# Whole float32 scores in twelve heads instead of eight, V's high parts on ACT, and the keys' low parts on GpSimd in an attention and mixer kernel

## The chip, the cores and the metric

The kernel runs on one core of one Trainium2 chip. Its time is the device time of one execution in microseconds (us); the time before is the median of three runs. One profiled execution was traced, and all spans, busy times and waits are from that execution. In the profile's rows PE is TensorE's matmuls, PEld its weight loads, DVE is VectorE, ACT is ScalarE, POOL is GpSimd, and SP is the engine whose queue issues the DMAs.

## The reference

Eight batches of eight heads go through block-causal attention (576 positions, 64 wide, blocks of 64), and the result x through a token mixer of rank 32 and a two-layer channel mixer:

```
scores = q @ k.T / 8;  masked where block_i < block_j
attn   = softmax(scores);  x = attn @ v          # heads side by side: 576 x 512 per batch
u      = x + (x.T @ U @ V).T
out    = u + relu(u @ w_ch1) @ w_ch2             # w_ch1 512 x 2048, w_ch2 2048 x 512
```

All inputs are float32. U, V, w_ch1 and w_ch2 arrive as 64-bit words and are converted on the chip.

## The kernel before

**Two ways to multiply.** A float32 matmul on PE runs as two passes, and the trace shows two MATMUL records for each. A matmul in the type float32r is one pass with a coarser mantissa. To keep accuracy, an operand is split into a high part (a copy to float32r) and a low part (the operand minus its high part), and several float32r products are summed in PSUM.

**Attention, head by head.** `split_qk` (lines 855 to 892) fetches q and k of one head, transposed, into `raw` (two buffers, so that a buffer serves every second head). Heads below FS = 8 use `raw` as it is: ACT multiplies the keys by 1/8 in place (line 874), and `softmax` makes the scores with whole float32 matmuls (line 931). From head 8 on, q and k are fetched twice, into both halves of the partitions (lines 859 and 861). ACT copies q's high part (line 877) and k's, scaled (line 878). GpSimd subtracts q's high part in the upper half (line 880). DVE multiplies k by 1/8 again and subtracts its high part into `k2` (line 885), and a DMA copies q's high part into `q2` (line 892). The scores are then two float32r matmuls a tile (lines 935 and 936). The mask is in the upper halves of q2 and k2, put there once by line 867 while heads FS-2 and FS-1 are prepared.

The scores of a head fill five tiles of 576, 448, 320, 192 and 64 columns. DVE takes the maxima (line 949), ACT the exponentials with their sums (line 960), and GpSimd scales by the inverse sums (line 986). PE transposes (line 1019). Heads below FP = 10 multiply with V in whole float32 (line 1061). Later heads split the transposed scores (lines 996 and 1038) and use V in parts: `split_v` makes the high part on GpSimd (line 904) and the low part there too (line 907), and line 1077 multiplies. `mix` (from line 1089) adds the token mixer after each second head.

**The weights.** `split64` converts 20 pieces of U, V, w1 and w2 during the first heads: one ACT pass, four DVE passes (lines 331, 332, 337 and 345), then a high part on ACT (line 360) and a low part on GpSimd (line 361).

**The channel mixer.** `ffn_chunk` multiplies chunks of 288 tokens: line 465 for the first product and line 488 for the second, into two PSUM banks (`bf`), with ACT (line 470) and DVE (line 473) between them. Its matmuls have the lowest priority and are placed where attention leaves PE free, from head 10 on. The first two chunks run in two turns, each with half of the weights. After the last head come the rest of the chunks and then the block products (line 659).

**What sets the order.** All work is added to a `Plan` as tasks with an engine, an estimated duration, a priority and buffers. `issue` runs them through a list scheduler and writes each engine's instructions in the order that comes out; each engine then works strictly in that order. Tasks with the mark `port`, and all of GpSimd's, are never planned at the same time as each other. Head h has priorities from 1000 h on, its preparation comes 900 earlier than the head before it, and the last pieces of the weights have 9000 to 16000, so that one comes about with each head from 9 to 16. When durations or engines of tasks change, the whole order behind them changes.

Of the kernel before, what the change touches and what calls it, by code (L numbers as in the profile page):

```python
# [12 lines left out]
AF = mybir.ActivationFunctionType  # L13
ALU = mybir.AluOpType
# [3 lines left out]
S = 576  # L18
# [9 lines left out]
SCALE = 0.125  # L28
# [15 lines left out]

FP = 10

FS = 8

PB = (1, 1, 1, 2, 2)

# [189 lines left out]
def _act(n, sbuf=False):  # L240
    return (93 if sbuf else 52) + 0.833 * n


def _dve(n):
    return 69 + 1.042 * n
# [9 lines left out]
def attention_then_mixer(  # L255
# [10 lines left out]
    nc = tc.nc  # L266
# [8 lines left out]
    add = plan.add  # L275

    def f32(ap):
        return ap.bitcast(F32)
# [525 lines left out]
    for r in raw_r:  # L804
# [3 lines left out]
        for x, fill in ((qi, 1.0), (ki, NEG)):  # L808
            nc.gpsimd.affine_select(
                out=x[:, :, 1, :], in_=x[:, :, 1, :], pattern=[[-1, 4], [0, 64]], compare_op=ALU.not_equal,  # L810
# [44 lines left out]
    def split_qk(h, pr):  # L855
        raw, q1, k1, q2, k2 = (r[h % 2] for r in (raw_r, q1_r, k1_r, q2_r, k2_r))

        def fetch():
            nc.sync.dma_start(out=raw[0:64, :], in_=qk[h])
            if h >= FS:  # L860
                nc.sync.dma_start(out=raw[64:P, :], in_=qk[h])
# [9 lines left out]
        if h < FS:  # L871
# [3 lines left out]
            )  # L875
            return
        add("ACT", _act(S, True), pr, lambda: nc.scalar.copy(q1.ap, raw[:, 0:S]), [raw], [q1])
        add("ACT", _act(S, True), pr, lambda: nc.scalar.activation(k1.ap, raw[:, S : 2 * S], AF.Copy, scale=SCALE), [raw], [k1])
        add(
            "POOL", 1380, pr, lambda: nc.gpsimd.tensor_sub(q1[64:P, :], raw[64:P, 0:S], f32(q1[64:P, :])),  # L880
            [raw, q1], [q1],
        )
        add(
            "DVE", _dve(S), pr,
            lambda: nc.vector.scalar_tensor_tensor(
                out=k2[0:64, :], in0=raw[0:64, S : 2 * S], scalar=SCALE, in1=f32(k1[0:64, :]),
                op0=ALU.mult, op1=ALU.subtract,
            ),
            [raw, k1], [k2], port=True,
        )  # L890

        add("SP", 600, pr, lambda: nc.sync.dma_start(out=f32(q2[0:64, :]), in_=f32(q1[0:64, :])), [q1], [q2], after=DL)
# [1 line left out]
    def split_v(h, pr):  # L894
        s = h % 2
        raw, vs = vr_r[h // 2 % 2], vs_r[s]
        if s == 0:
            add("SP", 910, pr, lambda: nc.sync.dma_start(out=raw.ap, in_=v[h // 2]), writes=[raw], after=DL)
        if h < FP:
            return  # L900
        hi, lo = vs[:, :, 0:64], vs[:, :, 64:P]
        add(
            "POOL", 430, pr,
            lambda: nc.gpsimd.tensor_scalar(out=hi, in0=raw[:, s], scalar1=1.0, scalar2=1.0, op0=ALU.mult, op1=ALU.mult),
            [raw], [vs],
        )
        add("POOL", 820, pr, lambda: nc.gpsimd.tensor_sub(lo, raw[:, s], f32(hi)), [raw, vs], [vs])
# [249 lines left out]
    for h in range(NH):  # L1157
        pr = 1000.0 * h
# [79 lines left out]
```

## Time and profile before

| what | us |
|---|---|
| median of 3 runs | 1201.78 (1198.8 to 1202.18) |
| profiled execution, device time | 1201.04 |
| profiled execution, span from first to last instruction | 1199.2 |

The profile's first two parts, its groups of instructions and its views by stretch are read as follows. Busy time of an engine is the time in which at least one of its instructions ran. A row of a group gives line, engine, operation, tiles (out<-in), shape and count, then busy us and the mean ns of one, then the idle time just before these instructions and what ended it. The view of one line gives the shortest, median and longest duration in ns. In the timeline a row has the start, the duration, the instruction, and in brackets the idle time before it. A row of waits gives the waiting instruction, what it waited for, the total us, how often, and the longest.

### The profile page before, as it was taken

Reading aid. Unit: us, or ns where it says so; the run is one execution under the profiler, and the core shown is the slowest. Engines: PE = TensorE matmul, PEld = TensorE weight load, DVE = VectorE, ACT = ScalarE, POOL = GpSimd, SP = SyncE. Lnnn points to the kernel's source line nnn. Section 1 sums busy time; section 2 is a strip of 40 time slices with the busy share of each in tenths; the row PEclk is TensorE's granted clock in tenths of the full one; section 3 lists DMA queues with packets and bytes.
Section 4 is the critical chain, followed back from the end, with each engine's and each line's share of the span. In section 5 each row is a group of like instructions: output and inputs, shape, how many; then the busy total and the mean of one; then the engine's idle time right before and its main releaser. Section 6 shows DMA issues by size and latency. Waiting matters only on the chain.

```text
span 1199.2 us, 25106 instructions
## 1 busy us (share of the span) xinstructions
PE 1169.1 (97%) x8970; PEld 1123.6 (94%) x8970; DVE 980.7 (82%) x2061; ACT 734.0 (61%) x1822; POOL 426.3 (36%) x588
## 2 busy tenths in 40 slices
PE   7989998999999999999999999999999999999998
PEld 5657888999999999999999999999999999999998
DVE  6879899888988898888887488425989889889887
ACT  6878686777878787878786344213544544544443
POOL 4558766665656566665654112210000000000000
PEclk9999999999999999999999999999999999999999
DMA  4465656535364535354532343211231231231221
GB/s 127 146 172 155 188 166 166 139 97 156 81 171 108 144 104 153 101 158 106 144 98 70 104 147 111 81 54 49 72 119 49 72 119 49 72 119 60 60 80 40
DMA packets 76428, 132.13 MB, mean 110 GB/s; under 512 B 9040, under 2 KB 53072, under 8 KB 76304
## 3 DMA queue, kind: packets, MB, share of 16 engines
q1 hardware_dynamic: 76304, 130.53, 38.8%
q8 instruction: 71, 1.16, 0.4%
q14 instruction: 53, 0.43, 0.1%
HBM read 92.75 MB, written 29.49 MB: 102 GB/s over the span
## 4 chain that ended last, share of the span: by engine, by line
PE 79%; DVE 11%; ACT 4%; issue 2%; DMA 2%; SPq 0%; POOL 0%; ACTq 0%; DVEq 0%; POOLq 0%
PE bb L659 29%; PE bf L465 10%; PE bf L488 10%; PE ba L1019 7%; PE ba L1077 5%; PE bg L465 4%; PE bg L488 4%; DVE mx L949 2%; DVE pl L1038 2%; ACT p L960 2%; PE ba L935 2%; PE ba L936 2%; PE ba L1061 1%; PE ba L1116 1%; PE ba L1102 1%
## 5 line engine op out<-in xcount | busy, mean ns | idle before, releaser
L986 POOL TENSOR_SCALAR p<-p,rv 128x192 f32<-128x192 f32 (+4 forms) x320 | 181.0, 580 | 150.5 <-DVE rv L977 92.7
L659 PE MATMUL bb<-hh,w1l 128*128 128x288 f32 x704 | 170.1, 295 | 0.0
L659 PE MATMUL bb<-hh,w1h 128*128 128x288 f32 x704 | 169.4, 295 | 0.0
L960 ACT ACTIVATE p<-ba,mx 128x448 f32<-128x448 f32 (+3 forms) x248 | 114.3, 466 | 22.2 <-DVE mx L949 18.9
L1019 PE MATMUL ba<-ident,p 128*128 128x128 f32 x768 | 123.5, 275 | 2.2 <-DVE pw L994 0.7
L1038 DVE TENSOR_TENSOR pl<-ba,ph 128x512 fp32r<-128x512 f32 x216 | 114.0, 550 | 11.7 <-ACT ph L996 9.2
L659 PE MATMUL bb<-hl,w1h 128*128 128x288 f32 x576 | 123.0, 295 | 0.1
L659 PEld LDWEIGHTS bb<-hh,w1l 128*128 128x128 f32 x704 | 122.9, 190 | 0.0
L659 PEld LDWEIGHTS bb<-hh,w1h 128*128 128x128 f32 x704 | 121.9, 188 | 0.0
L488 PE MATMUL bf<-hh,w2h 128*128 128x288 f32 x392 | 121.2, 309 | 0.0
L488 PE MATMUL bf<-hl,w2h 128*128 128x288 f32 x392 | 116.4, 297 | 0.0
L488 PE MATMUL bf<-hh,w2l 128*128 128x288 f32 x392 | 115.6, 295 | 0.0
L996 ACT CAST ph<-ba 128x512 fp32r<-128x512 f32 x216 | 100.5, 493 | 23.1 <-PE ba L1019 18.3
L447 POOL TENSOR_TENSOR ul<-ur,uh 128x288 fp32r<-128x288 f32 x72 | 63.3, 907 | 129.7 <-PE bf L465 72.6
L613 ACT CAST hh<-hb 128x576 fp32r<-128x576 f32 x98 | 65.9, 672 | 60.6 <-PE bb L659 58.1
L949 DVE TENSOR_REDUCE mx<-ba 128x1 f32<-128x448 f32 (+3 forms) x248 | 94.1, 407 | 10.0 <-PE ba L936 5.4
L1019 PEld LDWEIGHTS ba<-ident,p 128*128 128x128 f32 x768 | 90.5, 141 | 7.9 <-issue 4.5
L880 POOL TENSOR_TENSOR q<-raw,q 64x576 fp32r<-64x576 f32 x56 | 82.6, 1475 | 29.1 <-issue 9.2
L659 PEld LDWEIGHTS bb<-hl,w1h 128*128 128x128 f32 x576 | 91.9, 188 | 0.4 <-DVE hl L614 0.4
L1077 PE MATMUL ba<-ph,vs 128*128 128x256 f32 (+3 forms) x432 | 90.7, 263 | 0.1
L465 PE MATMUL bf<-uh,w1l 128*128 128x288 f32 x392 | 80.8, 303 | 0.0
L488 PEld LDWEIGHTS bf<-hh,w2l 128*128 128x128 f32 x392 | 74.9, 191 | 0.2
(167 smaller groups left out, 3288.1 us busy)
## 6 DMA issues: line engine op xcount, KB each, us to landing
raw<-in_qk_dram SPq DMA_DIRECT2D x120, 288.0 KB, 4.4
st<-in_w_dram SPq DMA_DIRECT2D x32, 512.0 KB, 3.6
o_d<-ot SPq DMA_DIRECT2D x72, 144.0 KB, 2.1
vr<-in_v_dram SPq DMA_DIRECT2D x32, 320.0 KB, 3.4
ur<-u_d SPq DMA_DIRECT2D x64, 144.0 KB, 3.0
whole<-o_d SPq DMA_DIRECT2D x32, 288.0 KB, 3.2
out_dram<-whole SPq DMA_DIRECT2D x32, 288.0 KB, 2.2
ur<-u_d SPq DMA_DIRECT2D x30, 288.0 KB, 3.2
```

The lines of the kernel that those rows point to most:

```text
L465: nc.tensor.matmul(ps[:, :T], w()[wn][:, k, fs], m[k].ap, start=(i == 0), stop=(i == len(ops) - 1))
L488: nc.tensor.matmul(ps[:, :T], w()[wn][:, f, ms], hs[f][x].ap, start=(i == 0), stop=(i == len(ops) - 1))
L613: add("ACT", _act(2 * T, True), E, lambda: nc.scalar.copy(h.ap, x[0]()), [x[1]], [h])
L659: nc.tensor.matmul(bank[:, i, :T], x()[:, w(k)], p.ap[:, k, :], start=first and n == 0, stop=last and n == len(ops) - 1)
L880: "POOL", 1380, pr, lambda: nc.gpsimd.tensor_sub(q1[64:P, :], raw[64:P, 0:S], f32(q1[64:P, :])),
L949: lambda i=i, at=at: nc.vector.tensor_reduce(out=mx[: P if i else 64, i : i + 1], in_=view(i, at), op=ALU.max, axis=AX.XY if wide else AX. ...
L960: nc.scalar.activation(out.rearrange("p (j k) -> p j k", j=2) if wide else out, view(i, at), AF.Exp, bias=mx[:rows, i : i + 1], accum_out= ...
L986: lambda x=x, rows=rows, i=i: nc.gpsimd.tensor_scalar(out=x, in0=x, scalar1=rv[:rows, i : i + 1], scalar2=1.0, op0=ALU.mult, op1=ALU.mult),
L996: add("ACT", _act(n), pr, lambda: nc.scalar.copy(out(), inp()), reads, writes)
L1019: nc.tensor.transpose(out=bank[:, a : a + P], in_=pt_r[i][h % PB[i]][:, j * P : (j + 1) * P], identity=perm.ap)
L1038: "DVE", _dve(m), pr, lambda: nc.vector.tensor_sub(pl[:, low], bank[:, :m], f32(ph[:, low])), [bank, bh], [bl]
L1077: nc.tensor.matmul(bank[0 : c.stop, a:n], vs[:, j, c], x[:, _at(g, j)], start=(i == 0), stop=(i == len(ops) - 1))
```

## The change

Three things are changed. First, FS goes from 8 to 12: heads 8 to 11 also take whole float32 scores from `raw`, and the mask is copied while heads 10 and 11 are prepared. Second, in the heads from 12 on ACT multiplies the keys by 1/8 in place in `raw`, as it does in the early heads, then copies the high part; the low part is now a plain subtraction, and GpSimd does it instead of DVE. Third, V's high part is an ACT copy and not a GpSimd multiplication by one. Lines behind 903 stand one line higher than before.

```diff
-FS = 8
+FS = 12
...
         add("ACT", _act(S, True), pr, lambda: nc.scalar.copy(q1.ap, raw[:, 0:S]), [raw], [q1])
-        add("ACT", _act(S, True), pr, lambda: nc.scalar.activation(k1.ap, raw[:, S : 2 * S], AF.Copy, scale=SCALE), [raw], [k1])
+        add(
+            "ACT", _act(S, True), pr,
+            lambda: nc.scalar.activation(raw[:, S : 2 * S], raw[:, S : 2 * S], AF.Copy, scale=SCALE), [raw], [raw],
+        )
+        add("ACT", _act(S, True), pr, lambda: nc.scalar.copy(k1.ap, raw[:, S : 2 * S]), [raw], [k1])
         add(
             "POOL", 1380, pr, lambda: nc.gpsimd.tensor_sub(q1[64:P, :], raw[64:P, 0:S], f32(q1[64:P, :])),
             [raw, q1], [q1],
         )
         add(
-            "DVE", _dve(S), pr,
-            lambda: nc.vector.scalar_tensor_tensor(
-                out=k2[0:64, :], in0=raw[0:64, S : 2 * S], scalar=SCALE, in1=f32(k1[0:64, :]),
-                op0=ALU.mult, op1=ALU.subtract,
-            ),
-            [raw, k1], [k2], port=True,
+            "POOL", 1380, pr, lambda: nc.gpsimd.tensor_sub(k2[0:64, :], raw[0:64, S : 2 * S], f32(k1[0:64, :])),
+            [raw, k1], [k2],
         )
...
         add(
-            "POOL", 430, pr,
-            lambda: nc.gpsimd.tensor_scalar(out=hi, in0=raw[:, s], scalar1=1.0, scalar2=1.0, op0=ALU.mult, op1=ALU.mult),
+            "ACT", _act(320, True), pr, lambda: nc.scalar.copy(hi, raw[:, s]),
             [raw], [vs],
         )
```

The order on the engines changes from the first heads on. Three places show it. The first is PE where split scores begin. Before, these are the rows around head 8's widest tile (`bw`; `k_0_147` and `q_0_145` are k1 and q1, the others k2 and q2):

```order
L1019 MATMUL ba_96<-ident,p_1_138 128x128
L1019 MATMUL ba_96<-ident,p_1_140 128x128 x2
L935 MATMUL bw<-k_0_147,q_0_145 128x288
L936 MATMUL bw<-k_0_128,q_0_126 128x288
L935 MATMUL bw<-k_0_147,q_0_145 128x288
L936 MATMUL bw<-k_0_128,q_0_126 128x288
L1061 MATMUL ba_98<-pw_144,vr_150 64x256 x3
```

Now they begin at head 12, and these rows lead to them:

```order
L465 MATMUL bf_91<-ul_112,w1h_199 128x288
L465 MATMUL bf_91<-ul_113,w1h_199 128x288
L488 MATMUL bf_90<-hh,w2h_201 128x288
L488 MATMUL bf_90<-hh,w2l_202 128x288
L488 MATMUL bf_90<-hl,w2h_201 128x288
L488 MATMUL bf_90<-hh,w2h_201 128x288
L488 MATMUL bf_90<-hh,w2l_202 128x288
L488 MATMUL bf_90<-hl,w2h_201 128x288
L934 MATMUL bw<-k_0_147,q_0_145 128x288
L935 MATMUL bw<-k_0_128,q_0_126 128x288
L934 MATMUL bw<-k_0_147,q_0_145 128x288
L935 MATMUL bw<-k_0_128,q_0_126 128x288
```

The first split scores of the program stood behind transposes alone; now 18 matmuls of the channel mixer, 12 of line 465 and 6 of line 488, stand right ahead of them.

The second place is DVE at the end of the weights' conversion, whose last pass on a piece is line 345. Before, these rows hold the last piece, next to head 17's widest maxima (`mx_154<-bw`):

```order
L331 TENSOR_SCALAR z_103<-z_103 128x512
L332 TENSOR_SCALAR z_103<-z_103 128x512
L1038 TENSOR_TENSOR pl_159<-ba_95,ph_157 128x256
L949 TENSOR_REDUCE mx_154<-bw 128x1
L337 SCALAR_TENSOR_TENSOR z_103<-st_101,z_103 128x512
L1085 TENSOR_TENSOR xt_164<-ba_98,tmp_161 64x256
L1038 TENSOR_TENSOR pl_159<-ba_95,ph_157 128x320
L345 SCALAR_TENSOR_TENSOR z_103<-st_101,z_103 128x512
```

Now the last piece stands among the work of head 14:

```order
L331 TENSOR_SCALAR z_103<-z_103 128x512
L332 TENSOR_SCALAR z_103<-z_103 128x512
L948 TENSOR_REDUCE mx_153<-ba_98 128x1
L1084 TENSOR_TENSOR xt_163<-ba_95,tmp_161 64x256
L948 TENSOR_REDUCE mx_153<-ba_98 64x1
L1037 TENSOR_TENSOR pl_159<-ba_97,ph_157 128x256
L337 SCALAR_TENSOR_TENSOR z_103<-st_101,z_103 128x512
L494 TENSOR_TENSOR ot<-bf_90,ur_105 128x288
L1037 TENSOR_TENSOR pl_159<-ba_95,ph_157 128x320
L975 TENSOR_REDUCE rv_155<-ss_132 128x3
L976 RECIPROCAL rv_155<-rv_155 128x3
L345 SCALAR_TENSOR_TENSOR z_103<-st_101,z_103 128x512
```

Its last pass moved from row 373 of DVE's order to row 321, three heads earlier, with the mixer's line 494 already beside it.

The third place is ACT in the heads with split scores. Before, this is how the two passes of a head's q and k stand between exponentials (line 960):

```order
L960 ACTIVATE p_0_136,ss_133<-ba_97,mx_154 128x320
L877 CAST q_1_146<-raw_131 128x576
L878 ACTIVATE k_1_148<-raw_131 128x576
L960 ACTIVATE p_0_135,ss_133<-ba_95,mx_154 128x192
L960 ACTIVATE p_0_134,ss_133<-ba_95,mx_154 64x64
L960 ACTIVATE p_0_139,ss_132<-bw,mx_153 128x576
```

Now there are three of them and the copy of V's high part (`vs`):

```order
L877 CAST q_0_145<-raw_130 128x576
L880 ACTIVATE raw_130<-raw_130 128x576
L995 CAST ph_157<-ba_97 128x320
L959 ACTIVATE p_0_134,ss_132<-ba_95,mx_153 64x64
L882 CAST k_0_147<-raw_130 128x576
L1082 COPY tmp_161<-ba_98 64x256
L995 CAST ph_157<-ba_97 128x256
L959 ACTIVATE p_0_136,ss_132<-ba_96,mx_153 128x320
L959 ACTIVATE p_0_135,ss_132<-ba_95,mx_153 128x192
L470 ACTIVATE hh<-bf_90 128x288
L1082 COPY tmp_162<-ba_98 64x320
L903 CAST vs_152<-vr_149 128x5x64
```

The exponentials and the copies of the transposed scores have two more instructions a head between them in ACT's queue.

## The prediction

> **What bounds the kernel now.** I read the engine shares of the page first, then a table of four stretches, then the chain of work inside the second and third of them.
>
> ```profile
> span 1199.2 us, 25106 instructions
> PE 1169.1 (97%) x8970; PEld 1123.6 (94%) x8970; DVE 980.7 (82%) x2061; ACT 734.0 (61%) x1822; POOL 426.3 (36%) x588
> ```
>
> TensorE is busy for 1169.1 of 1199.2 us. If its work stays the same, at most 30 us of its idle time can be won, and what it is given extra comes on top unless idle time takes it. So I ask where it idles. Columns: stretch, length, then busy us and instructions of PE, PEld, DVE, ACT, POOL, the granted clock, DMA.
>
> ```profile
> 0.00:100.00 100.00, 86.05 (x475) 58.51 (x476) 75.86 (x197) 76.87 (x213) 53.21 (x78) 1.00 0.55 146
> 100.00:200.00 100.00, 90.97 (x687) 84.94 (x686) 92.90 (x210) 75.12 (x204) 70.79 (x88) 0.95 0.59 168
> 200.00:675.00 475.00, 472.05 (x3899) 460.64 (x3899) 398.49 (x1034) 367.38 (x1054) 281.48 (x404) 1.00 0.45 120
> 675.00:1200.00 525.00, 520.01 (x3915) 519.54 (x3913) 413.42 (x623) 214.62 (x354) 20.82 (x20) 1.00 0.27 83
> ```
>
> From 200 us to 675 us PE idles 475 - 472.05 = 2.95 us, and after 675 us next to nothing but the end of the program (5 us). Before 200 us it idles 14.0 and 9.0 us, and in the second hundred its clock was 0.95, another 5 us of PE time. In that second hundred the busiest engine beside it is DVE, 92.9%.
>
> ```profile
> by line: DVE mx L949 10.0%; issue 7.8%; DVE pl L1038 7.0%; ACT p L960 6.1%; PE bf L488 5.2%; DVE z L332 5.1%; DVE z L345 4.6%; DMA raw<-in_qk_dram 3.6%; DVE k L885 3.6%; DVE z L331 3.5%; PE ba L1019 3.4%; PE ba L1077 3.4%; DVE xt L1085 2.9%
> ```
>
> This is the chain from 85 to 200 us. DVE heads it; the removed line, L885, is 3.6% of 115 us = 4.1 us of it, and the conversion of the weights (L331, L332, L345) 13.2% = 15 us. The same view from 200 to 675 us starts with PE lines:
>
> ```profile
> by line: PE bf L465 19.1%; PE bf L488 17.4%; PE ba L1019 14.0%; PE ba L1077 12.8%; PE ba L936 3.8%; PE ba L935 3.8%; issue 2.5%; ACT p L960 2.4%; PE ba L1116 2.4%; DVE pl L1038 2.4%; DVE mx L949 2.3%; PE ba L1102 2.2%; PE bw L936 1.8%; PE b
> ```
>
> There the mixer's matmuls (L465, L488) fill every gap that attention leaves. They could not fill the worst gap, from 175 to 190 us:
>
> ```profile
> 174.74 0.30 PE L488 MATMUL bf<-hl,w2h 128*128 128x288 f32 x1
> ...
> 176.60 0.33 PE L1019 MATMUL ba<-swap,p 128*128 128x128 f32 x1 [0.61 <-ACT p L960]
> ...
> 189.06 0.33 PE L1019 MATMUL ba<-swap,p 128*128 128x128 f32 x1 [1.39 <-ACT p L960]
> ...
> 190.02 0.38 PE L488 MATMUL bf<-hh,w2h 128*128 128x288 f32 x1
> ```
>
> No row of L465 or L488 stands between 174.74 and 190.02 us: the second product of the chunk waited for the last pieces of w2, which DVE was still converting, and the two banks were held by its sums. So the bound is DVE up to about 200 us and PE after it.
>
> **The change part by part.** The sum is made against the profiled execution's own 1201.04 us (its span and 1.8 us around it), 0.74 us under the median 1201.78.
>
> *Heads 8 to 11 on whole float32 scores (dearer on PE).* One head before, in float32 pieces:
>
> ```profile
> 53.93 1.14 PE L931 MATMUL bw<-raw 128*128 128x288 f32 x4
> 54.90 0.92 PE L931 MATMUL bf<-raw 128*128 128x448 f32 x2
> 55.65 0.27 PE L1102 MATMUL ba<-ident,xt 128*64 128x128 f32 x1
> ...
> 59.76 1.29 PE L931 MATMUL ba<-raw 128*128 128x320 f32 x6
> 60.98 0.44 PE L1019 MATMUL ba<-swap,p 128*128 128x128 f32 x2
> ```
>
> From start to the next start: 0.97 + 0.75 + 1.22 = 2.94 us. The same tiles in split form:
>
> ```profile
> 102.44 0.47 PE L935 MATMUL ba<-k,q 128*128 128x448 f32 x1
> ...
> 103.54 0.77 PE L465 MATMUL bf<-uh,w1h 128*128 128x288 f32 x4
> ...
> 105.78 0.38 PE L935 MATMUL bw<-k,q 128*128 128x288 f32 x1
> ...
> 106.39 0.70 PE L465 MATMUL bf<-uh,w1h 128*128 128x288 f32 x4
> ```
>
> 1.10 + 0.61 = 1.71 us. So 1.23 us a head, four heads: **+4.9 us** of PE. Ends: 0, if the idle time of heads 8 to 11 takes all of it, and 4.9.
>
> *The step from whole to split scores moves from head 8 to head 12.*
>
> ```profile
> PE bw L936 <- DMA q<-q: 3.1, 1, 3.1
> ```
>
> At head 8 PE stands 3.1 us for the copied high parts of q, with no mixer work yet in its queue. At head 12 the order shows a bank of L465 and a group of L488 right ahead of those scores: **-3.1 us**. Ends: 0, if that copy lands as late again (the mixer's 18 matmuls ahead last 2.4 us), and -3.1. The mask copies (L867) move from heads 6 and 7 to 10 and 11, four DVE instructions; I count them at nothing, since these heads also lose their four float32r splits on DVE.
>
> *Keys' low parts leave DVE.*
>
> ```profile
> L885 DVE SCALAR_TENSOR_TENSOR k<-raw,k x56: 718/752/1910, 70.7 to 633.4; 64x576 fp32r<-64x576 f32 x56
> L885 DVE SCALAR_TENSOR_TENSOR k<-raw,k 64x576 fp32r<-64x576 f32 x8 | 7.2, 901 | 0.7 <-ACT k L878 0.6
> L332 DVE TENSOR_SCALAR z<-z 128x512 int32<-128x512 int32 x9 | 7.5, 836 | 0.3
> L331 DVE TENSOR_SCALAR z<-z 128x512 f32<-128x512 f32 x9 | 7.3, 808 | 0.1
> ```
>
> The last three rows are the groups of 100 to 200 us. Eight L885 make 7.2 us there, 4.1 of them on the chain. The order shows what that does: the last piece of w2 is finished behind head 14's wide reduction, not behind head 17's, so the filler does not dry up. To be won are the 9.0 us of PE idle time and the 5 us of slow clock, 14 us in all. I take **-9 us**: the 7.2 us, and some 2 us of clock that go with the gaps. Ends: 0 and -14.
>
> Here a rule of the Trainium skill speaks against the change. In 100 to 200 us the two conversion steps lasted 808 and 836 ns with POOL 70.8% busy; from 700 to 775 us, with POOL nearly idle, they lasted:
>
> ```profile
> L331 DVE TENSOR_SCALAR z<-z 128x512 f32<-128x512 f32 x11 | 5.9, 533 | 4.2 <-ACT z L353 4.1
> L332 DVE TENSOR_SCALAR z<-z 128x512 int32<-128x512 int32 x11 | 5.2, 471 | 0.4
> ```
>
> So something of GpSimd's costs DVE about 0.3 us an instruction. The Trainium skill, "SBUF — State Buffer", section "Who interferes with whom", says why: a VectorE instruction in a two-port mode, or with two SBUF inputs, and a GpSimd instruction that reads SBUF take one shared pair of ports as a lock, and the later one waits for all of the other. The trace agrees in direction, 808 and 836 against 533 and 471 ns. By it the new subtractions can hold up the weights' conversion; it is a rival below.
>
> *What ACT and GpSimd get, from head 12 on.*
>
> ```profile
> L880 POOL TENSOR_TENSOR q<-raw,q x56: 1396/1426/1993, 70.5 to 633.9; 64x576 fp32r<-64x576 f32 x56
> L904 POOL TENSOR_SCALAR vs<-vr x54: 449/457/642, 104.2 to 646.6; 128x320 fp32r<-128x320 f32 x54
> L726 ACT ACTIVATE hb<-hb x48: 685/686/688, 844.2 to 1173.8; 128x576 f32<-128x576 f32 x48
> L445 ACT CAST uh<-ur x72: 417/432/458, 46.3 to 800.3; 128x288 fp32r<-128x288 f32 x72
> ```
>
> The new subtraction has the shape of L880: 1.43 us. The scaling in place has that of L726: 0.69 us. The high part of V on ACT has no row; between L445 (288 columns, 0.43 us) and L726 (576, 0.69 us), 320 columns come to 0.46 us. Some 44 heads lie between 200 and 675 us. ACT goes from 367.4 to 367.4 + 44 x 1.15 = 418 us, 88% of 475. POOL goes to 281.5 + 44 x (1.43 - 0.46) = 324 us, 68%. DVE loses 44 x 0.9 = 40 us: 358, 75%. So the busiest engine behind PE becomes ACT, 88%, where it was DVE, 84%. Behind ACT's longer queue stand the exponentials (L960), the float32r copies of the transposed scores (L996) and the mixer's L470. Behind POOL's stand the normalisations (L986); the new subtraction is queued right behind q's, and the q copy (3 us to landing) starts between the two, so both operands of L936 arrive together.
>
> *A buffer is freed later, and less is fetched.* The load of a head's q and k waits until its buffer is free, up to 220 us mostly for the removed line:
>
> ```profile
> SPq L859 <- DVE k L885: 17.0, 7, 4.7
> ```
>
> Now it waits for the second GpSimd subtraction, behind one more pass on ACT: 0.69 + 1.43 us later at most than where L885 stood. The buffer is for the head after next, some 10 us (475 us over 46 heads) ahead of need, so I count nothing; without that lead it is 2.1 us a head, and PE's filler stands before it. Heads 8 to 11 lose a second load, the copy of q, one ACT pass and a GpSimd subtraction each; none of it is on PE's path but by the wait counted above.
>
> From above, ACT's load costs what the second hundred paid: 9.0% PE idle with DVE at 92.9%, against 0.6% with DVE at 83.9%; on that line 88% makes 4.4%, 18 us more than now. From below it costs nothing, or wins the 2.95 us that are idle now. The row nearest in kind is this one, with filler at hand:
>
> ```profile
> 150.00:175.00 25.00, 24.32 (x200) 23.79 (x200) 24.17 (x60) 19.91 (x56) 16.69 (x22) 1.00 0.62 173
> ```
>
> DVE was busy 97%, yet PE idled 0.7 of 25 us. So I take **+1 us**. After 675 us nothing is touched.
>
> Sum: 1201.04 + 4.9 - 3.1 - 9 + 1 = **1194.8 us**.
>
> **The rivals.**
>
> *ACT sets the pace from 200 us (slower).* Its queue is in order, and its 88% leave waits for the scores and for the mixer's L470. The price is the 18 us above: 1194.8 - 1 + 18 = 1211.8 us. It decides once PE's idle time from 200 to 675 us is above some 13 us (2.95 and 10). For it: ACT waits on others already and cannot use all of the remaining 12%. Against it: the row of 150 to 175 us.
>
> *The second hundred regains nothing.* If the pace there is set by the fetches of raw and of w2 (the chain has 3.6% DMA raw), DVE's relief is idle time on DVE: 1201.04 + 4.9 - 3.1 + 1 = 1203.8 us. The change then does not do what its DVE part promises. Against it: DVE's 92.9%.
>
> *The lock.* If each new subtraction holds up a conversion step for its whole 1.43 us in heads 12, 13 and 14, 4.3 us of the 9 are gone: 1199.1 us. Against it: heads 8 to 11 lose 4 x 1.43 us of GpSimd subtractions in the same stretch.
>
> *All of it is regained.* All 14 us, and the 2.95 us: 1201.04 + 4.9 - 3.1 - 14 - 2.95 = 1185.9 us.
>
> **How the numbers follow.** About 0.3% (3.6 us) is what a measurement of this kernel tells from no change, so faster means below 1198.2 and slower above 1205.4. The forecast with its own range of 1190 to 1198: 0.50. All regained: 0.13. Nothing regained: 0.17. The lock: 0.06. ACT: 0.14. Faster 0.63, within 0.3% 0.23, slower 0.14. The range reaches from the full regain to the case without any: 1186 to 1204; ACT's case stays outside.
>
> **What would show it.** Right: from 100 to 200 us PE above 95 us busy and a clock near 1.00; no gap without L465 and L488 between 130 and 200 us; the wait of L936's successor for the copied q near zero; the float32 scores of heads 8 to 11 near 2.9 us each; PE idle under 5 us from 200 to 675 us, with ACT near 88%. Wrong: PE idle by over 13 us there, with waits that end on ACT; or a second hundred with PE near 91 us again although DVE is below 90%.

## The result, and the profile after

The changed kernel takes 1188.51 us (median of 4 runs, 1186.96 to 1189.59) against 1201.82 us for the kernel before (median of 4). The ratio is 0.9889 with a 95% interval of 0.9869 to 0.991, or 13.3 us less. The profiled execution took 1189.59 us, its span is 1187.8 us. It is the highest of the four.

The page of the changed kernel, span and busy time of each engine:

```profile
span 1187.8 us, 25058 instructions
PE 1166.8 (98%) x8970; PEld 1120.7 (94%) x8970; DVE 936.3 (79%) x2005; ACT 774.6 (65%) x1924; POOL 453.3 (38%) x582
```

PE is busy 2.3 us less than before although four heads have dearer scores; before, some 5 us of its busy time in the second hundred came from the lower clock. The same four stretches as in the prediction (stretch, length, busy us and instructions of PE, PEld, DVE, ACT, POOL, granted clock, DMA):

```profile
0.00:100.00 100.00, 89.91 (x482) 60.02 (x483) 78.51 (x204) 79.18 (x218) 52.56 (x80) 1.00 0.48 136
100.00:200.00 100.00, 95.74 (x747) 90.33 (x746) 84.68 (x204) 81.26 (x222) 70.69 (x83) 1.00 0.62 171
200.00:675.00 475.00, 472.53 (x3919) 462.26 (x3918) 366.39 (x987) 401.04 (x1136) 310.45 (x400) 1.00 0.45 123
675.00:1200.00 525.00, 508.57 (x3828) 508.10 (x3827) 406.69 (x613) 213.09 (x351) 19.59 (x20) 1.00 0.26 78
```

PE's idle time falls from 14.0 to 10.1 us in the first hundred, from 9.0 to 4.3 us in the second, where the clock is now 1.00 instead of 0.95, and from 2.95 to 2.5 us up to 675 us. By 675 us PE has done so much more that it is busy 11.4 us less after it (508.57 against 520.01): the program's end comes 11.4 us earlier (1187.8 against 1199.2).

The view of line 345, the last DVE pass on a piece of the weights, for the kernel before and then for the changed kernel (shortest, median and longest in ns, first and last start in us):

```profile
L345 DVE SCALAR_TENSOR_TENSOR z<-st,z x20: 170/681/1273, 12.1 to 186.1; 128x512 int32<-128x512 int32 x16, 96x288 int32<-96x288 int32 x2, 128x128 int32<-128x128 int32 x1, 128x32 int32<-128x32 int32 x1
```

```profile
L345 DVE SCALAR_TENSOR_TENSOR z<-st,z x20: 173/673/1803, 11.9 to 158.3; 128x512 int32<-128x512 int32 x16, 96x288 int32<-96x288 int32 x2, 128x128 int32<-128x128 int32 x1, 128x32 int32<-128x32 int32 x1
```

The weights are complete 28 us earlier, and the mixer no longer runs dry: between 120 and 215 us the longest stretch in which no matmul of lines 465 and 488 starts is 3.51 us (165.71 to 169.22), where it was 15.3 us (174.74 to 190.02). PE's waits of the changed kernel in its first 200 us, the three longest (waiting instruction, what it waited for, total us, times, longest):

```profile
PE bw L930 <- ACT raw L874: 6.2, 2, 5.4
PE ba L1018 <- ACT pw L995: 2.0, 2, 1.3
PE ba L1018 <- DVE xt L1084: 1.6, 1, 1.6
```

The wait for the copied q is gone. The 5.4 us lie at the start of the program.

### The profile page after: what moved, and what is told of

Read it like the earlier page. It is cut to its first block, busy times and chain, and to the rows that moved or that the text cites. A ratio compares the mean times of both kernels' runs of the same rounds, so it can differ in the third digit from the quotient of the medians.

```text
span 1187.8 us, 25058 instructions
## 1 busy us (share of the span) xinstructions
PE 1166.8 (98%) x8970; PEld 1120.7 (94%) x8970; DVE 936.3 (79%) x2005; ACT 774.6 (65%) x1924; POOL 453.3 (38%) x582
## 4 chain that ended last, share of the span: by engine, by line
PE 73%; DVE 4%; ACT 3%; issue 1%; DMA 0%; POOL 0%; ACTq 0%; DVEq 0%
PE bb L659 29%; PE bf L465 10%; PE bf L488 8%; PE ba L1018 5%; PE ba L1076 5%; PE bg L488 4%; PE bg L465 4%; PE ba L935 1%; PE ba L934 1%; ACT p L959 1%; DVE mx L948 1%; PE ba L1115 1%; PE ba L1101 1%; PE bw L934 1%; PE bw L935 1%
## 5 line engine op out<-in xcount | busy, mean ns | idle before, releaser
L985 POOL TENSOR_SCALAR p<-p,rv 128x192 f32<-128x192 f32 (+4 forms) x320 | 172.0, 552 | 165.6 <-DVE rv L976 70.9
L959 ACT ACTIVATE p<-ba,mx 128x448 f32<-128x448 f32 (+2 forms) x248 | 114.8, 467 | 19.7 <-DVE mx L948 13.3
L1037 DVE TENSOR_TENSOR pl<-ba,ph 128x512 fp32r<-128x512 f32 x216 | 114.2, 551 | 16.3 <-ACT ph L995 13.2
L488 PE MATMUL bf<-hl,w2h 128*128 128x288 f32 x384 | 113.5, 296 | 0.0
L488 PE MATMUL bf<-hh,w2l 128*128 128x288 f32 x384 | 112.7, 294 | 0.0
L995 ACT CAST ph<-ba 128x512 fp32r<-128x512 f32 x216 | 99.6, 494 | 11.6 <-PE ba L1018 10.5
L948 DVE TENSOR_REDUCE mx<-ba 128x1 f32<-128x448 f32 (+3 forms) x248 | 94.4, 408 | 10.5 <-PE ba L935 4.6
L884 POOL TENSOR_TENSOR q<-raw,q 64x576 fp32r<-64x576 f32 x52 | 74.0, 1423 | 12.2 <-DMA vr<-in_v_dram 2.6
L888 POOL TENSOR_TENSOR k<-raw,k 64x576 fp32r<-64x576 f32 x52 | 74.4, 1431 | 4.4 <-ACT k L882 1.1
```

The source lines that it names most:

```text
L488: nc.tensor.matmul(ps[:, :T], w()[wn][:, f, ms], hs[f][x].ap, start=(i == 0), stop=(i == len(ops) - 1))
L888: "POOL", 1380, pr, lambda: nc.gpsimd.tensor_sub(k2[0:64, :], raw[0:64, S : 2 * S], f32(k1[0:64, :])),
L948: lambda i=i, at=at: nc.vector.tensor_reduce(out=mx[: P if i else 64, i : i + 1], in_=view(i, at), op=ALU.max, axis=AX.XY if wide else AX. ...
L959: nc.scalar.activation(out.rearrange("p (j k) -> p j k", j=2) if wide else out, view(i, at), AF.Exp, bias=mx[:rows, i : i + 1], accum_out= ...
L985: lambda x=x, rows=rows, i=i: nc.gpsimd.tensor_scalar(out=x, in0=x, scalar1=rv[:rows, i : i + 1], scalar2=1.0, op0=ALU.mult, op1=ALU.mult),
L995: add("ACT", _act(n), pr, lambda: nc.scalar.copy(out(), inp()), reads, writes)
```

## The experiments

All were timed beside the kernel before. The table gives each run's ratio to it with its 95% interval, and of each profile PE's idle time in three stretches (the stretch less PE's busy time; the clock in brackets where it is under 1.00), DVE's and GpSimd's busy time from 100 to 200 us, and the last start of line 345. The differences between rows below are differences of these ratios times 1201 us; the kernel before was timed anew each time (medians 1199.71 to 1201.82 us), so differences of medians come out up to 2.3 us apart from them. The "loss" of PE in some of the expectations (41 us before 200 us, 23 us from 200 to 675 us) is another count than the idle time of the table (23.0 and 3.0 us), and how it was made is not shown.

| run | ratio | idle 0-100 | idle 100-200 | idle 200-675 | DVE, POOL 100-200 | last L345 |
|---|---|---|---|---|---|---|
| before | | 14.0 | 9.0 (0.95) | 3.0 | 92.9, 70.8 | 186.1 |
| the change | 0.9889 (0.9869 to 0.991) | 10.1 | 4.3 | 2.5 | 84.7, 70.7 | 158.3 |
| FS = 12 alone | 0.9929 (0.9902 to 0.9955) | 10.9 | 3.3 | 4.2 | 90.7, 67.3 | 168.0 |
| keys alone | 1.0035 (1.0021 to 1.0049) | 14.8 (0.97) | 13.5 (0.91) | 2.6 | 83.9, 72.4 | 184.0 |
| V alone | 1.0043 (1.0023 to 1.0063) | 12.4 (0.98) | 7.4 (0.97) | 6.3 | 91.1, 67.7 | 182.4 |
| keys and V | 1.0017 (1.0007 to 1.0026) | 13.9 (0.97) | 12.2 (0.97) | 2.1 | 86.9, 72.2 | 181.7 |
| FS = 12 and keys | 0.9882 (0.9867 to 0.9897) | 9.8 | 3.4 | 1.3 | 84.9, 75.8 | 155.0 |
| other order, before | 0.9975 (0.9964 to 0.9987) | 14.5 | 8.5 (0.98) | 2.0 | 94.0, 71.4 | 184.2 |
| other order, changed | 0.9917 (0.9902 to 0.9931) | 13.2 | 3.5 (0.98) | 2.2 | 86.6, 76.1 | 170.5 |

### Each part of the change alone

The whole score step moved to head 12, and nothing else:

```diff
-FS = 8
+FS = 12
```

> Only FS = 12; keys and V as before. Theory (DVE's work during the weights' conversion sets the loss on PE before 200 us): heads 8 to 11 lose four of the eight L885 that stood between 100 and 200 us and GpSimd's subtractions, so about half of the 9.6 us that PE lost less in that stretch is won, and the wait for the copied q at head 8 goes; against that PE gets 5 us. Time 1195 to 1199 us, last conversion pass (L345) near 175 us instead of 186 us. Rival (the moves of the later heads' work off DVE carry the gain): 1202 to 1206 us, the price on PE with nothing regained. Rival (any rewriting of the order moves the time): no forecast, anything within 10 us.

The keys' part alone, with FS = 8 and V as before:

```diff
-        add("ACT", ..., nc.scalar.activation(k1.ap, raw[:, S : 2 * S], AF.Copy, scale=SCALE), [raw], [k1])
+        add("ACT", ..., nc.scalar.activation(raw[:, S : 2 * S], raw[:, S : 2 * S], AF.Copy, scale=SCALE), [raw], [raw])
+        add("ACT", ..., nc.scalar.copy(k1.ap, raw[:, S : 2 * S]), [raw], [k1])
...
-            "DVE", ..., nc.vector.scalar_tensor_tensor(out=k2[0:64, :], ...
+            "POOL", 1380, pr, lambda: nc.gpsimd.tensor_sub(k2[0:64, :], raw[0:64, S : 2 * S], f32(k1[0:64, :])),
```

> Only the keys' change (scaled in place by ACT, low part subtracted by GpSimd), FS = 8, V as before. Theory: all eight L885 of 100 to 200 us leave DVE, so most of the 9.6 us is won there with no 5 us of float32 scores; the wait of 3 us at head 8 stays or grows, since GpSimd now has two subtractions and V's high part. Time 1191 to 1196 us. Rival (FS carries the gain): 1199 to 1203 us, with the gap of 175 to 190 us still there. From 200 to 675 us PE idle stays under 5 us under the theory, with DVE near 77% and ACT near 82%.

V's high part on ACT alone, with FS = 8 and the keys as before:

```diff
-            "POOL", 430, pr,
-            lambda: nc.gpsimd.tensor_scalar(out=hi, in0=raw[:, s], scalar1=1.0, scalar2=1.0, op0=ALU.mult, op1=ALU.mult),
+            "ACT", _act(320, True), pr, lambda: nc.scalar.copy(hi, raw[:, s]),
```

> Only V's high part on ACT, FS = 8, keys as before. Theory: DVE's work is unchanged, so PE's loss before 200 us stays near 41 us (of 200) and the time at 1199 to 1203 us. Rival (GpSimd's use of the port that it shares with DVE sets the pace of the conversion): nine L904 of 0.46 us less between 100 and 200 us shorten the conversion passes L331 and L332 (808 and 836 ns there) and the time falls to 1195 us or less.

FS = 12 alone takes 1192.67 us, 8.5 us less than before. The keys alone take 1206.5 us, 4.2 us more, and V alone 1206.76 us, 5.2 us more. So two of the three parts lose time by themselves. None of these three times lies in a range that its expectation gave: FS = 12 alone came out better than forecast, the other two worse than both of their cases. The second hundred of FS = 12 alone:

```profile
100.00:200.00 100.00, 96.72 (x764) 91.79 (x764) 90.71 (x219) 78.47 (x216) 67.26 (x87) 1.00 0.61 175
```

and of the keys alone:

```profile
100.00:200.00 100.00, 86.53 (x611) 79.41 (x611) 83.85 (x174) 70.99 (x189) 72.42 (x85) 0.91 0.54 150
```

These two rows speak against the prediction's measure of the bound. With DVE still busy 90.7 us, PE is busy 96.7; with DVE relieved to 83.9 us, PE falls to 86.5 at a clock of 0.91. The profile of the keys alone is of the longest of its ten executions (1209.1 us, median 1206.5), so its 0.91 is low even for this kernel; but keys and V with FS = 8, profiled near its own median, has the same pattern (DVE 86.9 us, PE 87.8, clock 0.97). DVE's busy share does not say what holds PE there. DVE's timeline of the keys alone shows what does (start, us, instruction):

```profile
158.66 1.42 DVE L331 TENSOR_SCALAR z<-z 128x512 f32<-128x512 f32 x1
160.12 2.75 DVE L332 TENSOR_SCALAR z<-z 128x512 int32<-128x512 int32 x1
```

and GpSimd's timeline there:

```profile
159.87 1.50 POOL L888 TENSOR_TENSOR k<-raw,k 64x576 fp32r<-64x576 f32 x1
161.33 1.25 POOL L361 TENSOR_TENSOR w2l<-z,w2h 128x512 fp32r<-128x512 f32 x1
162.57 0.62 POOL L904 TENSOR_SCALAR vs<-vr 128x320 fp32r<-128x320 f32 x1
```

L332 lasts 0.47 us where GpSimd is quiet (the prediction's row of 700 to 775 us). Here it lasts 2.75 us: it begins while GpSimd is in the new subtraction (L888), stays through the one behind it, and ends 0.3 us after that one does (162.87 against 162.58). The groups of DVE in the second hundred say the same of all passes on these two lines, first for the keys alone, then for the changed kernel:

```profile
L332 DVE TENSOR_SCALAR z<-z 128x512 int32<-128x512 int32 x7 | 10.4, 1479 | 0.2
L331 DVE TENSOR_SCALAR z<-z 128x512 f32<-128x512 f32 x7 | 7.6, 1085 | 0.0
```

```profile
L332 DVE TENSOR_SCALAR z<-z 128x512 int32<-128x512 int32 x7 | 5.8, 823 | 0.2
L331 DVE TENSOR_SCALAR z<-z 128x512 f32<-128x512 f32 x7 | 3.4, 489 | 0.0
```

The kernel before had 836 and 808 ns, so the 14 passes here pay some 6.4 us more than there (7 x 0.64 and 7 x 0.28), nearly the 7.2 us of the eight L885 that left. The other two passes (L337 and L345) grew less, from 756 and 824 ns to 903 and 1003. Over all four passes from 100 to 200 us the mean is 858 ns before, 1110 with the keys alone and 1086 with keys and V and FS = 8; with FS = 12 alone it is 747 and in the changed kernel 798, where L337 and L345 are longer than before (931 and 1011 ns). This is the pattern of the prediction's third rival, seen on a larger scale than it was priced.

### How the parts go together

The keys and V together, without FS = 12 (the changed kernel with the first line of the diff undone):

```diff
-FS = 12
+FS = 8
```

> The change without FS = 12 (keys and V changed, eight whole heads). First theory (the load on DVE before 200 us): all L885 gone, 1190 to 1196 us. Second theory (the pair of ports that GpSimd and DVE's conversion passes share, and GpSimd's queue: heads 8 to 11 with split scores put 4 x 2.9 us of GpSimd subtractions among the conversion passes): the last pass of L345 stays at 180 us or later, the mean of L332 or L345 is near 1.2 us as in the run with the keys alone, the clock falls below 0.95 in the second hundred, and the time is 1202 to 1209 us.

FS = 12 and the keys, without V (the changed kernel with V's high part on GpSimd again):

```diff
-            "ACT", _act(320, True), pr, lambda: nc.scalar.copy(hi, raw[:, s]),
+            "POOL", 430, pr,
+            lambda: nc.gpsimd.tensor_scalar(out=hi, in0=raw[:, s], scalar1=1.0, scalar2=1.0, op0=ALU.mult, op1=ALU.mult),
```

> FS = 12 and the keys' change, V's high part on GpSimd as before. If V's move is worth nothing by itself, the time is the changed kernel's within the luck of an order: 1186 to 1192 us. If the move of V is what lets GpSimd take the second subtraction, GpSimd is above 73% busy from 200 to 675 us (it was 65% in the changed kernel) and the time is near that of FS = 12 alone, 1191 to 1196 us.

Without FS = 12, keys and V take 1202.39 us, 2.0 us more than before. That is in the range of its second theory, though the clock of the second hundred is 0.97 and not below 0.95. FS = 12 and the keys take 1186.36 us, the lowest of all; the interval overlaps that of the whole change, so V on ACT brings nothing here (0.8 us lost by the ratios, 2.2 by the medians). What a part is worth thus depends on the others: FS = 12 wins 8.5 us by itself, 18.4 us when the keys' part is there (1.0035 to 0.9882) and 15.4 us with keys and V (1.0017 to 0.9889). The keys' part costs 4.2 us with FS = 8 and wins 5.6 us with FS = 12 (0.9929 to 0.9882).

A stretch of keys and V with FS = 8 shows how a long DVE pass reaches PE. DVE:

```profile
106.30 3.68 DVE L345 SCALAR_TENSOR_TENSOR z<-st,z 128x512 int32<-128x512 int32 x1
109.90 0.41 DVE L993 COPY pw<-ba 128x256 f32<-128x256 f32 x1
```

GpSimd:

```profile
105.64 1.75 POOL L888 TENSOR_TENSOR k<-raw,k 64x576 fp32r<-64x576 f32 x1
107.35 1.26 POOL L361 TENSOR_TENSOR w1l<-z,w1h 128x512 fp32r<-128x512 f32 x1
108.57 0.86 POOL L906 TENSOR_TENSOR vs<-vr,vs 128x320 fp32r<-128x320 f32 x1
```

PE (in brackets the idle time before and what ended it):

```profile
111.01 3.67 PE L1060 MATMUL ba<-pw,vr 128*64 128x256 f32 x11 [3.04 <-ACT pw L995]
```

L345 lasts 3.68 us instead of some 0.67 and ends 0.55 us after L906 does. Behind it in DVE's queue stands the copy of head 9's transposed scores (L993), behind that ACT's part of the same tile (L995), and PE stands 3.04 us for it. With FS = 12 the subtractions L884 and L888 of heads 8 to 11 do not exist, and these heads lie, in the changed kernel, from 71 us (head 8's scores) to 121 us (head 12's), where 6 of the 20 pieces of the weights get their last pass on DVE.

### Is it GpSimd's share or DVE's that must leave heads 8 to 11?

The changed kernel, with two subtractions on GpSimd added back in each of heads 8 to 11 (their results go to q1 and k1, which no one reads in these heads):

```diff
+            if h >= 8:
+                for x, o in ((q1, 0), (k1, S)):
+                    add(
+                        "POOL", 1380, pr,
+                        lambda x=x, o=o: nc.gpsimd.tensor_sub(x[64:P, :], raw[64:P, o : o + S], raw[64:P, 0:S]), [raw], [x],
+                    )
             return
```

> The changed kernel with GpSimd's share of heads 8 to 11 put back: two subtractions of 64x576 a head (8 in all, 11.4 us of GpSimd), whose results nothing uses. Theory (what FS = 12 wins is that GpSimd's subtractions go from among the weights' conversion): the last pass of L345 comes 10 us or more later than 158 us, the passes L332 or L345 lengthen towards the 0.9 to 1.6 us of the runs with FS = 8 and the keys' change, and the time is 1193 to 1200 us. Rival (DVE's own load, the copied q or the order do it): 1186 to 1191 us.

The changed kernel, with one scaled subtraction on DVE added back in each of heads 8 to 11, in the form of the old L885 (also unread):

```diff
+            if h >= 8:
+                add(
+                    "DVE", _dve(S), pr,
+                    lambda: nc.vector.scalar_tensor_tensor(
+                        out=k1[0:64, :], in0=raw[0:64, S : 2 * S], scalar=SCALE, in1=raw[0:64, 0:S],
+                        op0=ALU.mult, op1=ALU.subtract,
+                    ),
+                    [raw], [k1], port=True,
+                )
             return
```

> The changed kernel with DVE's share of heads 8 to 11 put back: one scaled subtraction of 64x576 a head (4 in all, 3.6 us of DVE with their waits at the 0.9 us of the removed line), whose results nothing uses. If DVE's load in that stretch sets the loss, 2 to 4 us more than the changed kernel: 1190 to 1193 us. If GpSimd's share does it, within 2 us of the changed kernel: 1186.5 to 1190.5 us.

GpSimd's share back: 1197.27 us, ratio 0.9981 (0.9969 to 0.9993), 11 us of the gain gone (8.8 by the medians). DVE's share back: 1195.47 us, ratio 0.9957 (0.9938 to 0.9976), 8.2 us gone (7.0 by the medians), which is above what either theory expected of it. Neither adds a matmul. The first two stretches with GpSimd's share back:

```profile
0.00:100.00 100.00, 85.97 (x461) 57.46 (x461) 77.84 (x196) 76.18 (x212) 56.28 (x80) 1.00 0.45 129
100.00:200.00 100.00, 94.29 (x718) 86.01 (x717) 86.85 (x200) 79.73 (x215) 74.70 (x86) 1.00 0.64 175
```

Eight subtractions, 11.4 us of GpSimd by 1.43 us each, on an engine that is busy 53% and 71% there, take 3.9 us of PE's busy time in the first hundred and 1.5 us in the second. One place shows how. DVE:

```profile
90.81 1.47 DVE L345 SCALAR_TENSOR_TENSOR z<-st,z 128x512 int32<-128x512 int32 x1
92.63 1.22 DVE L331 TENSOR_SCALAR z<-z 128x512 f32<-128x512 f32 x1
93.88 1.37 DVE L332 TENSOR_SCALAR z<-z 128x512 int32<-128x512 int32 x1
```

GpSimd, where L880 are two of the subtractions given back:

```profile
90.59 1.14 POOL L880 TENSOR_TENSOR q<-raw 64x576 fp32r<-64x576 f32 x1
91.69 1.87 POOL L880 TENSOR_TENSOR k<-raw 64x576 fp32r<-64x576 f32 x1
93.64 1.32 POOL L361 TENSOR_TENSOR w1l<-z,w1h 128x512 fp32r<-128x512 f32 x1
```

The three passes last 4.06 us, where their medians in this run add up to 1.53, and PE idles 2.27 us up to 96.25 us for a DVE instruction (L1125) two places behind them. The conversion of the weights ends at 174.0 us instead of 158.3, and its passes on line 332 last 1075 ns on average from 100 to 200 us (823 in the changed kernel); over all four passes the mean is 851 ns against 798.

With DVE's share back the weights are done at 159.7 us, about as early as in the changed kernel. In its profile, which is of the longest of its five executions (1196.69 us), most of the loss is one collision. Lines behind 875 stand nine higher than in the changed kernel: L897 is the keys' subtraction, L915 V's, L1093 the old L1084. DVE:

```profile
176.77 6.18 DVE L337 SCALAR_TENSOR_TENSOR z<-st,z 128x512 int32<-128x512 int32 x1
...
183.35 0.42 DVE L1093 TENSOR_TENSOR xt<-ba,tmp 64x256 f32<-64x256 f32 x1
```

GpSimd:

```profile
175.79 1.43 POOL L897 TENSOR_TENSOR k<-raw,k 64x576 fp32r<-64x576 f32 x1
177.18 3.08 POOL L447 TENSOR_TENSOR ul<-ur,uh 128x288 fp32r<-128x288 f32 x4
180.23 0.85 POOL L915 TENSOR_TENSOR vs<-vr,vs 128x320 fp32r<-128x320 f32 x1
181.06 1.35 POOL L994 TENSOR_SCALAR p<-p,rv 128x576 f32<-128x576 f32 x2
```

PE:

```profile
179.09 0.30 PE L488 MATMUL bf<-hh,w2l 128*128 128x288 f32 x1
179.22 0.30 PE L488 MATMUL bf<-hl,w2h 128*128 128x288 f32 x1
183.82 0.53 PE L943 MATMUL ba<-k,q 128*128 128x192 f32 x1 [4.30 <-DVE xt L1093]
...
186.79 0.44 PE L488 MATMUL bf<-hh,w2l 128*128 128x288 f32 x1
187.03 0.44 PE L488 MATMUL bf<-hl,w2h 128*128 128x288 f32 x1
```

L337 here works on the next weights, those of the block products at the end, and reads two tiles in SBUF. It ends 0.54 us after the eighth GpSimd instruction in a row. PE stands 4.30 us, and then its matmuls follow each other at 0.24 us where they did at 0.13.

The same L337 in the changed kernel, from 174.63 us on, lasts 0.78 us. None of the four subtractions stands in this collision. They lie some 70 us ahead of it (L879, first to last start 71.0 to 104.6 us, 6.6 us in all). From 50 to 125 us PE is busy 69.2 us and has 428 matmul records with DVE's share back, against 70.3 us and also 428 in the changed kernel; with GpSimd's share back it is 67.1 us and 399. So GpSimd's share is shown to cost PE time beside the conversion, and DVE's only about 1 us; the rest of the 8.2 us lies later, most of it in this collision, and adding the four had rewritten the order there.

The order has a part in the gain too. What is issued on DVE ahead of the last L345 can be counted in each trace:

| run | DVE instructions ahead of the last L345 | its start, us | us an instruction |
|---|---|---|---|
| before | 373 | 186.1 | 0.50 |
| FS = 12 alone | 345 | 168.0 | 0.49 |
| the change | 321 | 158.3 | 0.49 |
| GpSimd's share back | 342 | 174.0 | 0.51 |
| DVE's share back | 323 | 159.7 | 0.49 |
| keys alone | 336 | 184.0 | 0.55 |
| keys and V | 336 | 181.7 | 0.54 |

With the keys' part and FS = 8 the weights are late because DVE's instructions take longer. But FS = 12 alone and the whole change bring them forward mostly by a nearer place in DVE's order, at nearly the pace of before: 28 and 52 instructions fewer, at 0.49 us each, make 13.7 of 18.1 us and 25.5 of 27.8 us. (Four of the 28 and at most ten of the 52 are the subtractions that left.) Of the 15.7 us that GpSimd's share costs the weights, 21 more instructions make 10.3. The order is the planner's, which never plans a task with the mark `port` beside one of GpSimd's, so work taken off either engine can move the conversion forward in the plan, whatever the chip does. A kernel with this work taken out and the old order kept was not run.

So FS = 12 does not win because one engine was full. It takes work of DVE and GpSimd from heads 8 to 11, and the weights are done earlier. How much of that comes from fewer passes that meet GpSimd and how much from the nearer place in the order stays open. That passes lengthen beside GpSimd is shown where the keys' part loses with FS = 8, and where GpSimd's share is given back.

The Trainium skill, "SBUF — State Buffer", section "Who interferes with whom", says that a DVE instruction with two SBUF inputs, or in a two-port mode, and a GpSimd instruction that reads SBUF take one pair of ports as a lock, and that the one that came later waits for all of the other. These rows agree that it waits, but for two to eight GpSimd instructions, not one (2.75, 3.68 and 6.18 us). L337 and L345 have two SBUF inputs; L332 has one, and no run shows its mode. That the ports are the cause is the page's word; the runs show the overlap and its price.

### Where the keys' part pays

The keys' part only from head 20 on, with FS = 8 and then with FS = 12, V as before (the old form stays for heads below 20):

```diff
+        if h >= 20:
...
+            add(
+                "POOL", 1380, pr, lambda: nc.gpsimd.tensor_sub(k2[0:64, :], raw[0:64, S : 2 * S], f32(k1[0:64, :])),
+                [raw, k1], [k2],
+            )
+        else:
...
```

> FS = 8, V as before, the keys' change only in the heads from 20 on; heads 8 to 19 keep the low part on DVE. Second theory (the loss of the run with the keys alone is made before 200 us, where conversion passes meet GpSimd's second subtraction): up to 200 us all is as before, so 1198 to 1203 us. Rival (the longer queues of ACT and GpSimd cost it from 200 us on): 1204 us or more, with the loss on PE from 200 to 675 us 4 us or more above the 23 of before.

> FS = 12, V's high part on GpSimd as before, the keys' change only in the heads from 20 on. The runs with the keys' change lost 19 to 21 us of PE time from 200 to 675 us, those without it 23 to 30. Theory (the keys' change wins its 4 to 6 us in the late heads, by DVE's lower load): the time of FS = 12 with the keys' change in all heads, 1184 to 1189 us, and a loss of 19 to 21 us there. Rival (it wins in heads 12 to 19, beside the weights): the time of FS = 12 alone, 1191 to 1195 us.

With FS = 8: 1195.64 us, ratio 0.9955 (0.9939 to 0.9972), so the keys' part wins 5.4 us when heads 8 to 19 are spared, where it lost 4.2 us with them. With FS = 12: 1191.99 us, ratio 0.9934 (0.9917 to 0.995), no gain over FS = 12 alone, where all heads from 12 on gave 5.6 us. The first is better than both of its cases, the second is its rival's. PE's idle time from 200 to 675 us was 1.0 us in the first (of an execution at 1200.61 us, the highest of its four) and 5.1 us in the second. The two runs contradict each other on where the keys' part pays, and this stays open.

### One more step of the same kind

FS = 16 and the keys, V as before:

```diff
-FS = 12
+FS = 16
```

> FS = 16 with the keys' change, V's high part on GpSimd as before. Four more heads leave the stretch of the conversion, at 5 us of PE for their float32 scores. In the run with FS = 12 and the keys' change PE loses 9 us from 100 to 200 us, where a stretch with filler loses 1 us each 25 us, so at most 5 us are left to win: 1186 to 1191 us, no faster than FS = 12. Rival (what FS = 8 to 12 won, 14 to 20 us, goes on): 1175 to 1182 us.

1191.56 us, ratio 0.9931 (0.9916 to 0.9945), 5.9 us more than with FS = 12 and the keys and 0.6 us above the forecast range. PE's idle time in the three stretches is 10.5, 2.7 and 1.0 us, 14.2 in all against 14.6 with FS = 12 and the keys: hardly any idle time is won any more, and four more heads of dearer scores are paid in full (1.23 us each by the prediction, 4.9 us; PE's busy time is 1171.2 us against 1165.4).

### How much is luck of the order

The same instructions in another order, by one number of the planner, first for the kernel before, then for the changed one:

```diff
-NEAR, DL = 130, 3000
+NEAR, DL = 130, 3100
```

> The kernel before, with one planning number changed: the planner counts 3100 ns for a DMA to land instead of 3000. No instruction is added, removed or put on another engine; the order alone is rewritten. Theory: within 4 us of before (1198 to 1206 us), since the amount of work on DVE before 200 us is the same. Rival (luck of the order): 6 us or more off, in either direction, with the gap of 175 to 190 us gone or moved although DVE's work is the same.

> The changed kernel with the planner counting 3100 ns for a DMA to land instead of 3000: no instruction added, removed or moved to another engine. The same step moved the kernel before by 3 us. Theory: within 4 us of the changed kernel, 1184 to 1193 us, last conversion pass before 170 us and no half clock before 1150 us. Rival (the 12 us are luck of the order): 1195 us or more.

1198.05 us and 1190.73 us: 3.0 us less than the kernel before, 3.4 us more than the changed one. So some 3 us of a time can belong to the order and to no part of the change; one other order of each kernel does not bound what a third would do. The gain of FS = 12 and the losses of the two runs with shares given back are well above 3 us, the 0.8 us between the change and FS = 12 with the keys is not, and the effects of V (5.2 us lost alone, 2.2 us won beside the keys with FS = 8, 0.8 us lost with FS = 12 and the keys) are near it.

## Why the prediction came out as it did

The direction and the range were right; the size was 13.3 us where 7 were forecast (1194.8 from 1201.8). Against the profiled execution it was 1189.59 instead of 1194.8 us, 5.2 us less. Where these lie shows when the span is split into PE's busy and idle time. PE's idle time in the whole execution was to fall by 3.1 + 7 - 1 = 9.1 us and fell by 9.1 (30.1 to 21.1); that the sum fits so well is luck: 8.6 of the 10.1 us came before 200 us, and 0.5 us were won behind it where 1 was to be lost. Its busy time was to grow by 2.9 us (4.9 of dearer scores less 2 of clock) and fell by 2.3. So all 5.2 us are busy time: 3 of them are clock, of which the forecast took 2 of 5 us, and some 2 us are not located (the profiles with FS = 12 and a clock of 1.00 up to 675 us have 1165.4 to 1168.8 us of it).

- **Heads 8 to 11 on float32 scores, +4.9 us:** right. Head 11's widest tile in the changed kernel takes 0.98 us from its start to the next (0.97 forecast):

```profile
101.99 1.14 PE L930 MATMUL bw<-raw 128*128 128x288 f32 x4
102.97 0.70 PE L930 MATMUL ba<-raw 128*128 128x320 f32 x2
```

  The two records of a whole float32 matmul are not two passes at the price of float32r: at 128x288 each takes 0.24 us from start to start, a float32r matmul 0.13, so the pair costs 3.7 times as much. Three of the four heads lie in the first hundred (heads 8 to 10 begin at 71, 77 and 93 us). PE was busy 3.9 us longer there and idled as much less; 3.1 us of that is the wait of the next term, which stood at 80.8 us.
- **The step to split scores behind the mixer, -3.1 us:** right. The row of that wait is gone, and the mixer's matmuls stand ahead of head 12.
- **The second hundred, -9 us:** right in size, wrong in its reason. 4.8 us of idle time and 5 us of clock came back, 9.8 us. But the prediction put it down to DVE's relief by eight L885, "So the bound is DVE up to about 200 us". The keys' part alone takes all of them away and loses; FS = 12 alone leaves DVE at 90.7% and regains as much (3.3 us idle, clock 1.00). What the prediction read from the order did come: the last piece of w2 is ready earlier and the filler does not dry up (3.51 us without it at most). But it is earlier mostly because 321 and not 373 instructions stand ahead of it on DVE, at 0.49 and 0.50 us each.
- **ACT and GpSimd from 200 us, +1 us:** wrong in sign, by 1.5 us. PE idled 2.5 us, not 4, and did 20 matmuls more in the same 475 us. ACT was busy 401 us (84%, forecast 88%), GpSimd 310 (324), DVE 366 (358). The new instructions themselves cost what was forecast (0.69, 1.43 and 0.46 us):

```profile
L880 ACT ACTIVATE raw<-raw x52: 672/687/712, 112.8 to 630.4; 128x576 f32<-128x576 f32 x52
```

```profile
L888 POOL TENSOR_TENSOR k<-raw,k x52: 1407/1426/1750, 114.8 to 632.9; 64x576 fp32r<-64x576 f32 x52
```

```profile
L903 ACT CAST vs<-vr x54: 446/458/492, 89.6 to 635.7; 128x320 fp32r<-128x320 f32 x54
```

- **ACT sets the pace (the slower rival):** did not come. The first of PE's waits of the changed kernel from 200 to 675 us is

```profile
PE ba L1130 <- ACT p L959: 0.8, 3, 0.3
```

  Its measure, the engine's share, was no better a guide than DVE's: V alone had ACT at 379 us, less than the changed kernel's 401, and PE idled 6.3 us:

```profile
200.00:675.00 475.00, 468.73 (x3851) 454.04 (x3850) 395.75 (x1033) 379.14 (x1090) 257.10 (x354) 1.00 0.44 121
```

  What stands out there is a wait on GpSimd for the copy that moved, in the waits of V alone from 200 to 675 us:

```profile
POOL vs L906 <- ACT vs L903: 22.5, 16, 3.9
```

  Before, both halves of V were GpSimd's own and needed no wait between engines. It is a candidate for these 6.3 us and was not tested by itself. But up to 675 us PE idles 26.1 us in all with V alone, against 25.9 before; its 5 us are in PE's busy time (1174.3 against 1169.1 us), and their cause stays open.
- **The lock (rival, 0.06):** the runs bear out that passes wait beside GpSimd, but not its place and price. It was looked for in heads 12 to 14 of the change and priced at 4.3 us against it. It shows in heads 8 to 11 when they have the keys' part: from 100 to 200 us the passes there last 1086 to 1110 ns on average, and the part loses; with these heads emptied they last 798.
- **All of it regained (1185.9 us):** the result lies nearer to this than to the forecast, 2.6 us above it by the median.
- **What the signs said:** PE above 95 us at a clock of 1.00 in the second hundred, the copied q's wait gone, and under 5 us idle up to 675 us all came. ACT came to 84% and not near 88%, and gaps without the mixer of up to 3.51 us were left between 130 and 200 us. "A second hundred with PE near 91 us again although DVE is below 90%" came too, in the kernels with the keys' part and FS = 8 (86.5 and 87.8 us) and with DVE's share back (90.7): the prediction named the sign of its own error, but a kernel with all parts at once could not show it.

## What to carry to other kernels

A busy share of 93% beside an idle PE doesn't make that engine the bound: look whether its instructions last longer than the same ones where another engine is quiet, and if so, take work away from that stretch rather than move it between the two engines. Dearer work on the main engine pays where it takes away waits of that engine, and stops paying when hardly any are left (FS = 12 wins, FS = 16 gives back 5.9 us). Where a planner writes the order, count how far a deadline moved in it before a gain is put down to the chip. Take a change of several parts apart: here one part carried the gain, one was worth -4 or +6 us depending on it, and one brought nothing.

## What was unexpected of the hardware

A DVE pass of 0.67 us stood through several GpSimd instructions in a row, up to 6.18 us; GpSimd did not let it in between. And a gap of PE does not by its length alone decide on the clock. In the kernel before, a gap of 1.72 us ahead of 123.52 us was followed by 3.4 us at half clock, and in the run with DVE's share back the gap of 4.30 us by 6.8 us of it (columns as in the stretches above; 0.51 and 0.50 are the clock):

```profile
123.80:127.20 3.40, 3.40 (x15) 3.28 (x15) 1.83 (x5) 1.40 (x3) 1.33 (x1) 0.51 0.35 104
```

```profile
183.60:190.40 6.80, 6.58 (x29) 6.49 (x30) 4.71 (x13) 4.83 (x13) 0.60 (x2) 0.50 0.07 23
```

With GpSimd's share back PE stood longer than 1.72 us ahead of this row, and the clock stayed at 1.00 in the whole first hundred:

```profile
96.25 0.52 PE L1024 MATMUL ba<-ident,p 128*128 128x128 f32 x3 [2.27 <-DVE tz L1125]
```
